# Decode attention on one core: keys transposed in place four groups at a time, and one load of the last value tile split by partitions

## The chip, the core and the metric

The kernel runs on one core of a Trainium2 chip. A core has a matrix engine (TensorE, PE in the profile, its weight loads PEld), a vector engine (VectorE, DVE), a scalar engine (ScalarE, ACT), GpSimd (POOL), and a queue engine (SyncE, SP) that here only issues transfers. Sixteen DMA engines move data between HBM and the on-chip memory SBUF, which has 128 partitions. The metric is the time of one execution in microseconds, taken as the median of several runs.

## The reference

One query token attends to 65,536 keys. There are 32 query heads and 8 key/value heads, so that four query heads share one key/value head; a head has 128 numbers, and everything is bf16.

```python
B, Hq, Hkv, Sq, Sk, D = 1, 32, 8, 1, 65536, 128
scores = jnp.einsum("bhqd,bhkd->bhqk", q, k) * D ** -0.5
p = softmax(scores, axis=-1)
out = jnp.einsum("bhqk,bhkd->bhqd", p, v)
```

Keys and values are 134 MB each. Each is read once, and there is little arithmetic for a byte.

## The kernel before

The outer loop runs over the key/value heads g. The 65,536 rows of a head are laid out so that partition p holds rows 512p to 512p+511. They come in four tiles (s = 0 to 3) of 128 rows for each partition, 4 MB a tile. A tile is one transfer: `k_load` (L118) and `v_load` (L196) each issue it from the SP queue. All tiles, of keys and of values, share one pool of four buffers (`iopool`), so a tile's load waits until the work on the tile four places earlier has let go of its buffer.

`k_step` (L124) computes the scores of one key tile. The 128 rows of a partition are seen as 16 chunks c of 8 groups w; the group w takes every eighth row. VectorE transposes blocks of 32 by 32 four-byte words, two groups in an instruction, out of the key tile `kn` into a tile `T` from a pool of three (L133 to L138). Four matmuls for each group (L144) read `T`; the 32 matmuls of a tile add up in one PSUM bank `sc`, which ScalarE copies out (L151). Since only the transposes read `kn`, the key buffer comes free when the last of the four transposes of a tile is done.

`softmax` (L153) follows the fourth key tile of a head: VectorE takes a maximum, TensorE and VectorE spread it, and ScalarE computes the exponentials. `transpose_weights` (L187) turns them on VectorE. The values of head g-1 are multiplied by them while the keys of head g come in: `v_stream` (L206) has 32 matmuls for a value tile, behind the 32 matmuls of the key tile in TensorE's queue. So the loads alternate between keys and values, except for four key tiles at the beginning and four value tiles at the end.

The last value tile is loaded in six pieces, of 64, 32, 16, 8, 4 and 4 rows for each partition, so that `finish_last` (L262) can work on a piece while the next one lands. After the last piece come a few small matmuls, one VectorE operation, and the store of 4 partitions, issued from ScalarE's queue (L250). There are two earlier stores of that kind, of 4 and of 3 rows for each of 4 partitions, and four loads of the queries of 32 partitions each (L70), on that queue too.

Buffers are given out, waits are put in and the order on each engine is chosen by a planner ahead of the run. It makes an instruction wait for an earlier one when their accesses to a tile conflict. Transfers count their completion on a rotation of semaphores.

Of the kernel before, what the change touches and what calls it, by code (L numbers as in the profile page):

```python
# [14 lines left out]
NW = 16  # L15
# [5 lines left out]
def kernel(  # L21
# [17 lines left out]
    nc = tc.nc  # L39
    P = nc.NUM_PARTITIONS  # L40
    B, Hq, Sq, D = q.shape
# [10 lines left out]
    fp32 = mybir.dt.float32  # L52
    bf16 = mybir.dt.bfloat16

    const = ctx.enter_context(tc.tile_pool(name="const", bufs=1))
    iopool = ctx.enter_context(tc.tile_pool(name="iopool", bufs=4))
    tpool = ctx.enter_context(tc.tile_pool(name="tpool", bufs=3))
    spool = ctx.enter_context(tc.tile_pool(name="spool", bufs=2))
    epool = ctx.enter_context(tc.tile_pool(name="epool", bufs=2))
    opool = ctx.enter_context(tc.tile_pool(name="opool", bufs=2))  # L60
# [14 lines left out]
    for x in range(2):  # L75
# [8 lines left out]
        out=sel[:, :], in_=ident[:, :].rearrange("p (x h) -> p h x", h=HPG), axis=AX.X, op=ALU.max  # L84
# [3 lines left out]
        out=blk[:, :], in_=ident[:, :].rearrange("p (j w h) -> p w j h", w=W, h=HPG), axis=AX.XY, op=ALU.max  # L88
# [35 lines left out]
    def k_step(g, s, kn):  # L124
        if s == 0:
            S_tiles[g] = spool.tile([P, KT, 4 * P], fp32, name="S_g")
        wq = Wq[g % 2]
        kv = kn[:, :, :].rearrange("p (c w) d -> p w c d", w=W)
        sc = psc.tile([P, 4 * P], fp32, name="sc")
        for w in range(W):  # L130
            if s == 0 and w == W // 2 and g > 0:
                transpose_weights(g - 1)
            if w % 2 == 0:  # L133
                T = tpool.tile([P, 2, NW, D], bf16, name="T")
                nc.vector.transpose(  # L135
                    out=T[:, :, :, :].bitcast(fp32),
                    in_=kv[:, w:w + 2].bitcast(fp32),
                )  # L138
            Tv = T[:, w % 2].rearrange("p n (b i r) -> p n b i r", b=2, r=2)
            for b in range(2):  # L140
                for r in range(2):
                    bp = 2 * b + r
                    at = bp * WX + 28 - 4 * w
                    nc.tensor.matmul(  # L144
                        out=sc[:, :],
                        lhsT=wq[:, at:at + P],
                        rhs=Tv[:, :, b, :, r],
                        start=(w == 0 and bp == 0),
                        stop=(w == W - 1 and bp == 3),
                    )  # L150
        nc.scalar.copy(out=S_tiles[g][:, s, :], in_=sc[:, :])  # L151
# [35 lines left out]
    def transpose_weights(g):  # L187

        ET = epool.tile([P, KT, NW, 32], bf16, name="ET")
        nc.vector.transpose(  # L190
            out=ET[:, :, :, :].rearrange("p s c x -> p (s c x)"),
            in_=E_tiles[g][:, :, :].rearrange("p s x -> p (s x)"),
        )
        ET_tiles[g] = ET

    def v_load(g, s, pieces=(NT,)):  # L196
        vb = iopool.tile([P, NT, D], bf16, name="vb", tag="io", align_bytes=2048)
        src = v[0, g].rearrange("(p n) d -> p n d", p=P)
        x = 0
        for step in pieces:  # L200
            n0 = s * NT + x
            nc.sync.dma_start(out=vb[:, x:x + step, :], in_=src[:, n0:n0 + step, :])  # L202
            x += step
        return vb

# [94 lines left out]
    for g in range(Hkv + 1):  # L300
        if 0 < g < Hkv:
            queries(g)
        for s in range(KT):
            if g < Hkv:
                k_step(g, s, k_load(g, s))
            elif s == 0:
                transpose_weights(g - 1)
            if g > 0:
                last = s == KT - 1
                if g == Hkv and last:  # L310
                    finish_last(g - 1, s, v_load(g - 1, s, pieces=(64, 32, 16, 8, 4, 4)))
                else:
                    v_stream(g - 1, s, v_load(g - 1, s), NT, last)
                    if last:
                        pick(g - 1)
                    if last and g % 4 == 0:
                        finish(g - 4, 4)
                    if last and g == Hkv - 1:
                        finish(g - g % 4, g % 4)
        if g < Hkv:  # L320
            softmax(g)
# [30 lines left out]
```

## Time and profile before

| | us |
|---|---|
| median of 3 runs | 631.95 (631.68 to 632.71) |
| profiled execution, its own time | 632.0 |
| profiled execution, span from first to last instruction | 630.1 |
| DMA, mean rate over the span | 427 GB/s |
| TensorE busy, share of the span | 58% |
| VectorE busy, share of the span | 54% |
| mean granted TensorE clock | 0.783 |

The span leaves out 1.9 us of the execution's own time. In the rows of instruction groups, a line names the source line, the engine, the operation, what it writes and reads, and the shape with the number of instructions; behind the bar stand busy time, the mean of one in nanoseconds, and the idle time ahead of them with what ended it. In the rows of stretches, the columns are the stretch and its length, busy time of five engines, the granted clock, the share of the DMA engines' time, and the rate.

### The profile page before, as it was taken

What the parts mean: (1) busy time and instruction counts of PE and PEld (TensorE: products, weight loads), DVE (VectorE), ACT (ScalarE), POOL (GpSimd) and SP (SyncE); (2) the same over time, 40 slices, a digit from 0 to 9 for tenths busy, and PEclk for the clock granted to TensorE, in tenths of its full rate; (3) what the DMA queues carried; (4) which work ended last, traced back from release to release, by engine and by line L of the source; (5) the groups of instructions that cost most, each with busy time, mean ns of one, the idle gap of its engine ahead of it and who ended that gap; (6) DMA issues with size and microseconds to landing.
All of it is one profiled execution on the core that took longest, in us unless ns stands there. A gap on an engine that the chain in (4) does not pass through costs nothing.

```text
span 630.1 us, 4872 instructions
## 1 busy us (share of the span) xinstructions
PE 363.2 (58%) x2134; PEld 141.8 (23%) x2134; DVE 340.0 (54%) x200; ACT 36.8 (6%) x49; POOL 6.4 (1%) x37
## 2 busy tenths in 40 slices
PE   0686836745457464575645856457665466644645
PEld 0232312212122221222211222112221122211212
DVE  0998834784337753377543675336754366553511
ACT  0000100010000100001000010001000010000100
POOL 0000000000000000000000000000000000000000
PEclk9998888767787677876778867788677787767866
DMA  8999999999999999999999999999999999999996
GB/s 368 433 434 431 433 432 431 432 433 433 434 433 432 435 433 434 433 432 433 434 435 435 432 427 432 437 432 433 433 432 433 434 433 433 432 433 434 431 425 263
DMA packets 10192, 268.78 MB, mean 427 GB/s; under 512 B 1340, under 2 KB 1596, under 8 KB 1852
## 3 DMA queue, kind: packets, MB, share of 16 engines
q1 hardware_dynamic: 9936, 268.44, 98.9%
q8 instruction: 16, 0.26, 0.1%
q10 hardware_dynamic: 236, 0.04, 0.0%
q14 instruction: 4, 0.03, 0.0%
HBM read 268.47 MB, written 0.01 MB: 426 GB/s over the span
## 4 chain that ended last, share of the span: by engine, by line
DMA 73%; DVE 11%; issue 10%; PE 4%; ACTq 0%; DVEq 0%; SPq 0%
DMA kn<-in_k_dram 66%; DVE T L135 11%; DMA vb<-in_v_dram 5%; PE sc L144 4%; DMA qn<-in_q_dram 2%; PE psum_o L213 0%; ACTq L70 0%; DVEq L135 0%; PE psum_f L280 0%; PE psum_oT L290 0%; SPq L202 0%; DVE wq L109 0%; PE psum_f L287 0%; PE psum_f L296 0%; DVE sel L83 0%
## 5 line engine op out<-in xcount | busy, mean ns | idle before, releaser
L144 PE MATMUL sc<-T,wq 128*128 128x512 bf16 x1024 | 288.1, 445 | 220.3 <-DVE T L135 220.3
L135 DVE STREAM_TRANSPOSE T<-kn 128x2048 f32<-128x2048 f32 x128 | 284.2, 2277 | 198.2 <-DMA kn<-in_k_dram 198.2
L144 PEld LDWEIGHTS <-wq 128*128 128x128 bf16 x1024 | 109.4, 109 | 394.9 <-issue 159.6
L213 PE MATMUL psum_o<-vb,ET 128*32 128x512 bf16 x1008 | 64.8, 402 | 12.3 <-DMA vb<-in_v_dram 10.1
L151 ACT COPY S_g<-sc 128x512 f32<-128x512 f32 x32 | 18.8, 587 | 511.0 <-PE sc L144 511.0
L213 PEld LDWEIGHTS <-ET 128*32 128x32 bf16 x1008 | 25.5, 100 | 49.2 <-issue 28.2
L156 DVE TENSOR_REDUCE mx<-S_g 128x1 f32<-128x2048 f32 x8 | 18.3, 2286 | 26.7 <-ACT S_g L151 26.7
L190 DVE STREAM_TRANSPOSE ET<-E_g 128x2048 bf16<-128x2048 bf16 x8 | 18.5, 2311 | 16.3 <-ACT E_g L177 16.3
L177 ACT ACTIVATE E_g<-S_g,nmb 128x2048 bf16<-128x2048 f32 x8 | 16.0, 2001 | 47.5 <-DVE nmb L174 40.4
L224 DVE TENSOR_TENSOR o_m<-psum_o,mask 128x512 f32<-128x512 f32 x8 | 5.5, 681 | 21.5 <-PE psum_o L213 21.5
L109 POOL COPY wq<-qx 32x16 bf16<-32x16 bf16 x28 | 5.3, 190 | 427.2 <-PE sc L144 410.2
L160 PE MATMUL psum_t<-ident,mx 128*1 128x128 f32 x8 | 2.2, 270 | 11.2 <-DVE mx L156 11.2
L100 DVE STREAM_TRANSPOSE qx<-qn 128x64 f32<-128x64 f32 x1 | 0.2, 245 | 15.2 <-DMA qn<-in_q_dram 15.2
L172 PE MATMUL psum_b<-one,mrow 1*128 1x1 f32 x16 | 3.6, 290 | 8.3 <-DVE mrow L166 8.3
L230 DVE TENSOR_REDUCE o_all<-o_m 128x128 f32<-128x512 f32 x8 | 8.0, 1000 | 0.0
L172 PEld LDWEIGHTS psum_b<-one,mrow 1*128 1x128 f32 x16 | 3.0, 235 | 12.1 <-issue 11.3
L237 PE MATMUL psum_l<-lsum_all,sel 128*4 128x4 f32 (+2 forms) x6 | 0.6, 166 | 7.7 <-ACT E_g L177 7.7
L257 PE MATMUL psum_f<-o_all,sel 128*4 128x512 f32 (+1 forms) x4 | 2.4, 705 | 2.9 <-DVE o_all L230 2.9
L160 PEld LDWEIGHTS psum_t<-ident,mx 128*1 128x1 f32 x8 | 0.6, 79 | 15.1 <-DVE mx L156 11.6
L244 DVE TENSOR_TENSOR o_out<-psum_f,rl 4x512 bf16<-4x512 f32 (+2 forms) x3 | 1.5, 501 | 3.6 <-PE psum_f L257 2.4
L290 PE MATMUL psum_oT<-ET,vb 128*128 128x4 bf16 x56 | 2.0, 167 | 1.6 <-DMA vb<-in_v_dram 1.6
L174 DVE COPY nmb<-psum_b 128x1 f32<-128x1 f32 x8 | 1.2, 152 | 3.0 <-PE psum_b L172 3.0
(28 smaller groups left out, 16.0 us busy)
## 6 DMA issues: line engine op xcount, KB each, us to landing
kn<-in_k_dram SPq DMA_DIRECT2D x32, 4096.0 KB, 29.6
vb<-in_v_dram SPq DMA_DIRECT2D x31, 4096.0 KB, 34.5
vb<-in_v_dram SPq DMA_DIRECT2D x1, 2048.0 KB, 29.5
vb<-in_v_dram SPq DMA_DIRECT2D x1, 1024.0 KB, 31.5
vb<-in_v_dram SPq DMA_DIRECT2D x1, 512.0 KB, 32.3
vb<-in_v_dram SPq DMA_DIRECT2D x1, 256.0 KB, 32.4
vb<-in_v_dram SPq DMA_DIRECT2D x2, 128.0 KB
qn<-in_q_dram ACTq DMA_DIRECT2D x4, 8.0 KB, 10.3
```

Source lines behind the costliest of these rows:

```text
L109: eng.tensor_copy(out=wv[qd, :, :, 32 * a + 28:32 * a + 28 + HPG], in_=qv[qd, :, :, g * HPG:(g + 1) * HPG],)
L135: nc.vector.transpose(out=T[:, :, :, :].bitcast(fp32), in_=kv[:, w:w + 2].bitcast(fp32),)
L144: nc.tensor.matmul(out=sc[:, :], lhsT=wq[:, at:at + P], rhs=Tv[:, :, b, :, r], start=(w == 0 and bp == 0), stop=(w == W - 1 and bp == 3),)
L151: nc.scalar.copy(out=S_tiles[g][:, s, :], in_=sc[:, :])
L156: nc.vector.tensor_reduce(out=mx[:, :], in_=S_g[:, :, :].rearrange("p n c -> p (n c)"), axis=AX.X, op=ALU.max)
L160: nc.tensor.transpose(out=psum_t[:, :], in_=mx[:, :], identity=ident[:, :])
L172: nc.tensor.matmul(out=psum_b[:, :], lhsT=mrow[:, :], rhs=one[:, :], start=True, stop=True)
L177: nc.scalar.activation(out=E_g[:, :, :].rearrange("p s x -> p (s x)"), in_=S_g[:, :, :].rearrange("p s x -> p (s x)"), func=ACT.Exp, bias= ...
L190: nc.vector.transpose(out=ET[:, :, :, :].rearrange("p s c x -> p (s c x)"), in_=E_tiles[g][:, :, :].rearrange("p s x -> p (s x)"),)
L213: nc.tensor.matmul(out=o_tiles[g][32 * j:32 * j + 32, :, :], lhsT=ET_tiles[g][:, s, c, :], rhs=vb[:, c * W + 4 * x:c * W + 4 * x + 4, :], ...
L224: nc.vector.tensor_tensor(out=o_m[:, :, :], in0=o_tiles[g][:, :, :], in1=mask[:, :].unsqueeze(2).broadcast_to([P, 4, D]), op=ALU.mult,)
L230: nc.vector.tensor_reduce(out=o_all[:, g, :], in_=o_m[:, :, :].rearrange("p x d -> p d x"), axis=AX.X, op=ALU.add)
```

## The change

The pool of `T` tiles goes. VectorE transposes four groups of a key tile in one instruction and writes them where it read them; the matmuls read the key tile itself. In the last value tile, the piece of 32 rows is loaded by five transfers in place of one: partitions 0 to 111, and then 112 to 115, 116 to 119, 120 to 123 and 124 to 127. No other transfer has 32 rows.

```diff
-    tpool = ctx.enter_context(tc.tile_pool(name="tpool", bufs=3))
...
         for w in range(W):
             if s == 0 and w == W // 2 and g > 0:
                 transpose_weights(g - 1)
-            if w % 2 == 0:
-                T = tpool.tile([P, 2, NW, D], bf16, name="T")
-                nc.vector.transpose(
-                    out=T[:, :, :, :].bitcast(fp32),
-                    in_=kv[:, w:w + 2].bitcast(fp32),
-                )
-            Tv = T[:, w % 2].rearrange("p n (b i r) -> p n b i r", b=2, r=2)
+            if w % 4 == 0:
+                groups = kv[:, w:w + 4].bitcast(fp32)
+                nc.vector.transpose(out=groups, in_=groups)
+            Tv = kv[:, w].rearrange("p n (b i r) -> p n b i r", b=2, r=2)
...
         for step in pieces:
             n0 = s * NT + x
-            nc.sync.dma_start(out=vb[:, x:x + step, :], in_=src[:, n0:n0 + step, :])
+
+            p0 = 0
+            for p1 in (112, 116, 120, 124, P) if step == 32 else (P,):
+                nc.sync.dma_start(out=vb[p0:p1, x:x + step, :], in_=src[p0:p1, n0:n0 + step, :])
+                p0 = p1
             x += step
```

## The prediction

> **What bounds the kernel now.** I read the rows of slices first, then the waits of the SP queue, then the groups, then the last microseconds.
>
> ```profile
> DMA  8999999999999999999999999999999999999996
> GB/s 368 433 434 431 433 432 431 432 433 433 434 433 432 435 433 434 433 432 433 434 435 435 432 427 432 437 432 433 433 432 433 434 433 433 432 433 434 431 425 263
> ```
>
> The DMA engines are busy in every slice, at 433 GB/s from the second on. 268.4 MB at 433 GB/s is 620 us of the 630.1 us span. Around it lie the first 1.7 us and the work after the last piece. So time is lost only by a hole in this stream, or at its end.
>
> ```profile
> L144 PE MATMUL sc<-T,wq 128*128 128x512 bf16 x1024 | 288.1, 445 | 220.3 <-DVE T L135 220.3
> L135 DVE STREAM_TRANSPOSE T<-kn 128x2048 f32<-128x2048 f32 x128 | 284.2, 2277 | 198.2 <-DMA kn<-in_k_dram 198.2
> ...
> kn<-in_k_dram SPq DMA_DIRECT2D x32, 4096.0 KB, 29.6
> vb<-in_v_dram SPq DMA_DIRECT2D x31, 4096.0 KB, 34.5
> ```
>
> VectorE idles 198.2 us for keys, so it isn't the bound. A 4 MB tile takes 9.7 us at 433 GB/s, yet a key load lands 29.6 us after its issue: two more tiles stand ahead of it in the queue. That is the cover for the first edit.
>
> ```profile
> 621.00:622.00 1.00, 0.94 (x16) 0.35 (x15) 0.00 (x0) 0.00 (x0) 0.00 (x0) 1.00 0.97 400
> 622.00:623.00 1.00, 0.10 (x4) 0.00 (x0) 0.81 (x2) 0.00 (x0) 0.00 (x0) 0.90 0.91 360
> 623.00:624.00 1.00, 0.51 (x19) 0.51 (x20) 0.90 (x1) 0.00 (x0) 0.00 (x0) 0.50 0.62 250
> 624.00:625.00 1.00, 0.79 (x29) 0.71 (x27) 0.00 (x0) 0.00 (x0) 0.00 (x0) 0.50 0.54 205
> 625.00:626.00 1.00, 1.00 (x22) 0.56 (x18) 0.00 (x0) 0.00 (x0) 0.00 (x0) 0.50 0.30 105
> ```
>
> The DMA share falls to a half before it falls to nothing: the engines don't end together. By the packets, seven end between 622.8 and 623.2 us, one at 624.6 and eight near 625.6. The second edit works on this.
>
> ```profile
> 592.38 32.29 DMA vb<-in_v_dram
> 624.67 0.05 issue
> 624.72 0.58 PE psum_oT L290 x16
> 625.30 0.52 PE psum_f L287 x2
> 625.82 0.30 PE psum_oT L290 x8
> 626.12 0.52 PE psum_f L280 x4
> ```
>
> In the chain that ended last, the piece of 16 rows lands at 624.7 us; from there TensorE's work follows without a gap. What delays that landing delays the end by as much.
>
> **Edit 1, transposes in place.** 128 instructions of 2.28 us go and 64 of twice the size come. Back to back the old ones stand 2.2 us apart (four in 8.89 us), so a new one takes about 4.4 us, from at least 2.3 us (no more than an old one) to 4.6 us (two old ones). VectorE's load of 284 us stays or falls a little: worth nothing, as its idle time is 198 us.
>
> What moves is when a key buffer comes free: no longer after the last transpose, but after the last matmul. At 188.8 us the four transposes take 8.9 us and the buffer is free at 197.7 us. After the change, 4.4 us + 4.4 us + 16 matmuls of 0.30 us (32 took 9.55 us) make 13.6 us: free at 202.4 us, 4.7 us later. Behind this load on SP stands the value load, whose buffer TensorE frees 1.9 us later. The next two loads give cover: a key load must reach the queue before the three tiles landing after its predecessor in the buffer are through, some 28 us after that one landed, and 14 us are used. Where a head begins, the weights' transpose (2.3 us) and the wait for exponentials add about 5 us, leaving 9 us. Tightest is the start: VectorE works through four key tiles until 53.5 us; then comes the first softmax. Two transposes and the maximum, each waited for, put the fifth tile's last matmul near 73.4 us instead of the release at 67.7 us. The load into its buffer must be moving at 80 us, when the three tiles behind the fifth are in; with 1.0 us from issue to moving 5.7 us are left. Cost: nothing. If that cover went, each microsecond beyond it would be a microsecond of DMA.
>
> The matmuls now read rows 2 KB apart instead of 256 bytes. No row shows this; bounded by equal speed and by the 631 ns that a value matmul takes at the half clock instead of 445 ns, a tile's 32 need 9.6 to 13.6 us, with 1.9 us of value matmuls still under the 19.4 us of two loads. I take equal speed, since the transposes already read this pitch at the rate of the packed ones. Cost: nothing either way.
>
> **Edit 2, five transfers for one.** SP issues four more, 0.43 us each, 1.7 us, about 20 us ahead of need. Completions go round eight semaphores, and a transfer waits for the one eight places before it:
>
> ```profile
> SPq L202 <- DMA out_dram<-o_out: 7.1, 1, 7.1
> SPq L202 <- DMA vb<-in_v_dram: 3.8, 2, 3.5
> ```
>
> With ten transfers for the last tile the ninth waits for the 64-row piece (621.1 us) and the tenth for the 112-partition transfer. A wake takes 0.4 us and an issue reaches the engines 1.0 us later, while a late engine has 2.2 us of 16, 8 and 4 rows left: 0.8 us of cover, cost nothing; without it, the shortfall.
>
> Engines: in the before, 236 packets stand on ScalarE's queue.
>
> ```profile
> q10 hardware_dynamic: 236, 0.04, 0.0%
> ```
>
> The query loads have 128 rows and the stores 16 + 12 + 4; 236 - 160 leaves 76 completions, which is 4 loads by 16 and 3 stores by 4. So a transfer of 4 partitions runs on four engines. Three of those are among the early seven and one is the engine that ends at 624.6 us (by the packets of the store at 600 us). At 433/16 = 27.1 GB/s for an engine, 8 KB take 0.31 us. The twelve others lose one packet in eight: -0.3 us. The four get 11 packets for 8: +0.9 us, so the one in between ends at 625.5 us. Best case: end 0.1 to 0.3 us earlier.
>
> That holds if the parts keep the full rate of every engine; no row has a transfer of 112 partitions or a large one of 4. The other end: the four small transfers, 128 KB, go at the rate of a single engine, 4.8 us, in place of 1.2 us: +3.6 us on top. The one in between, 1.0 us ahead, then ends 3.5 us late; the early three, 2.5 to 2.8 us ahead, 1.7 to 2 us late. If moreover the 112 partitions went at 205 GB/s, the rate with half the engines at work, their 0.92 MB would take 4.5 us for 2.1 us: +2.4 us, 5.9 us in all. Between -0.3 and +5.9 us I take +3.0 us, nearer the engine's rate than the full one: the only 4-partition transfers in the trace already leave twelve engines out. Sum: 632.0 + 0 + 3.0 = 635.0 us for the profiled execution, which stands at the median (631.95).
>
> [...]
>
> **The rivals.** *The tail stays as it is* (0.30): every engine keeps 27.1 GB/s whatever partitions it writes. For it: all engines run alike in 63 tiles. [...] Time 631.8 us. It decides as long as the small transfers lose less than 1.4 us on the engine in between, which ends at 625.5 us: beyond that the end is more than 1.3 us late.
>
> *The second transposes wait for the first 16 matmuls* (0.07), if the planner takes the interleaved groups for one region. The place is the second transpose of each key tile; a tile then takes 4.4 + 4.9 + 4.4 + 4.9 = 18.6 us on VectorE and TensorE in turn, decisive from 19.4 us on. At a head's start 4.6 us of maximum and weights come on top. 18.3 + 4 x 16.4 (full clock) + 28 x 18.6 + 7 x 4.6 + 25 us for the last values = 662 us.
>
> *Faster* (0.03): the engines even out. The mean of their ends is 624.3 us: at most 1.3 us, 630.7 us.
>
> **How the numbers follow.** Likeliest, with 0.60, is the split that costs: 635.0 us, own range 633.3 to 638. A change under 0.2% (1.3 us) can't be told from none here. Same 0.30, slower 0.60 + 0.07, faster 0.03. The range 631.5 to 638.2 leaves out the waiting transposes, the gain and the worst end.
>
> **What would show it.** The transpose row at 64 of about 4.4 us; key loads landing about 25 us after issue; DMA slices at 433 GB/s until 615 us; then a tail in which the DMA share sinks for longer and the 16-row piece lands near 628 us. I am wrong if slices before 600 us dip, if the transposes wait for matmuls, or if the tail ends at 625.5 us.

## The result, and the profile after

The changed kernel takes 636.86 us, the median of six runs, against 632.13 us for the kernel before. Five of the six lie between 635.97 and 637.12 us; the sixth, a disturbed one of 711.25 us, is not counted in the ratio, which is 1.0072 with a 95% interval of 1.0061 to 1.0084. The profiled execution took 636.67 us, its span is 634.9 us. So 4.7 us were lost, where 3.0 us had been forecast.

Over most of the span nothing changed. The slices of the changed kernel:

```profile
DMA  9999999999999999999999999999999999999996
GB/s 370 440 442 428 436 428 429 428 429 428 429 429 429 448 441 429 429 428 429 428 431 433 440 440 433 431 428 429 429 430 436 433 442 435 431 429 428 432 415 147
```

The rate stays near 433 GB/s up to slice 38 and there is no hole; only the last two slices are poorer, 415 and 147 instead of 425 and 263 GB/s. The groups and the landing of the key loads show that the first edit did what it says:

```profile
L140 PE MATMUL sc<-kn,wq 128*128 128x512 bf16 x1024 | 286.4, 445 | 224.0 <-DVE kn L134 222.8
L134 DVE STREAM_TRANSPOSE kn<-kn 128x4096 f32<-128x4096 f32 x64 | 280.2, 4418 | 189.9 <-DMA kn<-in_k_dram 189.9
...
kn<-in_k_dram SPq DMA_DIRECT2D x32, 4096.0 KB, 24.0
```

64 transposes take 4.42 us each, 280 us together for 284 us before. A matmul takes 445 ns as before. The key loads land 24.0 us after issue instead of 29.6 us: they are issued later, and the queue ahead of them is still longer than one tile.

The loss lies in the last 18 us. Stretches of the kernel before (first fence) and of the changed one (second); the last two columns are the share of the DMA engines' time and the rate:

```profile
616.00:618.00 2.00, 1.80 (x20) 0.82 (x23) 0.00 (x0) 0.00 (x0) 0.00 (x0) 0.50 0.91 389
618.00:620.00 2.00, 1.66 (x20) 0.56 (x13) 0.00 (x0) 0.00 (x0) 0.00 (x0) 0.66 1.12 477
620.00:622.00 2.00, 0.94 (x16) 0.35 (x15) 0.00 (x0) 0.00 (x0) 0.00 (x0) 1.00 0.88 362
```

```profile
616.00:618.00 2.00, 1.50 (x16) 0.69 (x19) 0.00 (x0) 0.00 (x0) 0.00 (x0) 0.50 0.97 414
618.00:620.00 2.00, 2.00 (x20) 0.70 (x13) 0.00 (x0) 0.00 (x0) 0.00 (x0) 0.50 1.08 266
620.00:622.00 2.00, 0.10 (x4) 0.00 (x0) 0.00 (x0) 0.00 (x0) 0.00 (x0) 0.78 1.21 219
622.00:624.00 2.00, 0.00 (x0) 0.00 (x0) 0.00 (x0) 0.00 (x0) 0.00 (x0) 1.00 0.75 168
624.00:626.00 2.00, 1.47 (x16) 0.49 (x15) 0.00 (x0) 0.00 (x0) 0.00 (x0) 0.57 0.99 188
626.00:628.00 2.00, 0.43 (x4) 0.00 (x0) 1.49 (x2) 0.00 (x0) 0.00 (x0) 0.50 0.81 198
```

From 618 us on, the engines are busy and move half as much. Packet by packet the same is seen: in the kernel before, every packet of 8 KB near the end takes 309 ns; in the changed one they take 0.31 to 1.09 us, mostly near 0.6 us. The 64-row piece, a transfer that was not changed, has 128 packets of 16 KB; 35 of them rise in the same microseconds from 611 ns to between 0.80 and 1.77 us.

TensorE, in order of time, first before and then after:

```profile
621.06 1.05 PE L213 MATMUL psum_o<-vb,ET 128*32 128x512 bf16 x16 [1.40 <-DMA vb<-in_v_dram]
623.49 1.01 PE L290 MATMUL psum_oT<-ET,vb 128*128 128x4 bf16 x32 [1.39 <-DMA vb<-in_v_dram]
624.72 0.58 PE L290 MATMUL psum_oT<-ET,vb 128*128 128x4 bf16 x16 [0.21 <-DMA vb<-in_v_dram]
```

```profile
624.53 1.90 PE L213 MATMUL psum_o<-vb,ET 128*32 128x512 bf16 x16 [4.43 <-DMA vb<-in_v_dram]
628.96 1.42 PE L290 MATMUL psum_oT<-ET,vb 128*128 128x4 bf16 x48 [2.53 <-DMA vb<-in_v_dram]
```

The 64-row piece is there 3.5 us later, the 32-row piece 5.5 us later. The last packet of the 16-row piece ends at 629.2 us, while the matmuls of the 32 rows run, so the 48 matmuls of both go without a gap. From there the work is the same as before.

### The profile page after: what moved, and what is told of

Read it like the earlier page. It is cut to its first block, busy times and chain, and to the rows that moved or that the text cites. A ratio compares the mean times of both kernels' runs of the same rounds, so it can differ in the third digit from the quotient of the medians.

```text
span 634.9 us, 4750 instructions
## 1 busy us (share of the span) xinstructions
PE 361.7 (57%) x2134; PEld 141.8 (22%) x2134; DVE 336.3 (53%) x136; ACT 36.8 (6%) x49; POOL 6.4 (1%) x37
## 3 DMA queue, kind: packets, MB, share of 16 engines
q1 hardware_dynamic: 9952, 268.44, 99.0%
## 4 chain that ended last, share of the span: by engine, by line
DMA 63%; PE 22%; DVE 14%; issue 0%; ACTq 0%; DVEq 0%; SPq 0%
DMA kn<-in_k_dram 55%; PE sc L140 21%; DVE kn L134 14%; DMA vb<-in_v_dram 5%; DMA qn<-in_q_dram 2%; PE psum_o L213 0%; PE psum_oT L290 0%; ACTq L69 0%; PE psum_f L280 0%; DVE wq L108 0%; PE psum_f L287 0%; PE psum_f L296 0%; DVE sel L82 0%; DVEq L134 0%; SPq L201 0%
## 5 line engine op out<-in xcount | busy, mean ns | idle before, releaser
L140 PE MATMUL sc<-kn,wq 128*128 128x512 bf16 x1024 | 286.4, 445 | 224.0 <-DVE kn L134 222.8
L134 DVE STREAM_TRANSPOSE kn<-kn 128x4096 f32<-128x4096 f32 x64 | 280.2, 4418 | 189.9 <-DMA kn<-in_k_dram 189.9
L213 PEld LDWEIGHTS <-ET 128*32 128x32 bf16 x1008 | 25.3, 100 | 53.3 <-issue 29.6
```

The lines of the kernel that those rows point to most:

```text
L134: nc.vector.transpose(out=groups, in_=groups)
L140: nc.tensor.matmul(out=sc[:, :], lhsT=wq[:, at:at + P], rhs=Tv[:, :, b, :, r], start=(w == 0 and bp == 0), stop=(w == W - 1 and bp == 3),)
L213: nc.tensor.matmul(out=o_tiles[g][32 * j:32 * j + 32, :, :], lhsT=ET_tiles[g][:, s, c, :], rhs=vb[:, c * W + 4 * x:c * W + 4 * x + 4, :], ...
```

## The experiments

Three accounts were to be told apart. By the first, the split is the whole cost, since the parts of a split transfer hinder each other where they are written into SBUF; that is a supposition, as the trace shows no packet's partition. By the second, the cost is one of counts: more transfers, and later ones that wait for the completion of earlier ones. By the third, the transposes in place carry a part of it, since they hold the key buffers longer. All kernels were compared with the kernel before on the same chip.

**Each edit alone.** The first kernel has the transposes in place and the one transfer of before; the second has separate `T` tiles and the split.

```diff
 e1_inplace, against the changed kernel
-            p0 = 0
-            for p1 in (112, 116, 120, 124, P) if step == 32 else (P,):
-                nc.sync.dma_start(out=vb[p0:p1, x:x + step, :], in_=src[p0:p1, n0:n0 + step, :])
-                p0 = p1
+            nc.sync.dma_start(out=vb[:, x:x + step, :], in_=src[:, n0:n0 + step, :])
```

> The transposes in place alone; the 32-row piece is one transfer of 128 partitions again. My theory (the split is the whole cost): the time of the kernel before within 0.2%, 631.5 to 633.0 us, with the DMA rate in the last microseconds as before (324 to 477 GB/s between 616 and 622 us). Rival (a part of the loss comes from the buffers held longer, which may make loads late): 633.5 us or more, with slices under 430 GB/s well before the tail.

> The split of the 32-row piece alone; the transposes write into separate tiles as before. My theory: the whole loss, 636 to 637.5 us, with packets of 8 KB near 0.6 us instead of 0.31 us and a tail at about 200 to 270 GB/s between 618 and 628 us although the engines are busy. Rival (in-place transposes carry part of it): below 635.5 us.

The first took 631.79 us, 0.9999 of the kernel before (0.9990 to 1.0008). The second took 636.68 us, 1.0075 (1.0063 to 1.0088). The third account falls, and the first edit is worth nothing measurable in either direction. The tail of the second kernel has the half rate with busy engines again:

```profile
618.00:620.00 2.00, 1.73 (x19) 0.50 (x9) 0.00 (x0) 0.00 (x0) 0.00 (x0) 0.54 1.04 246
620.00:622.00 2.00, 0.00 (x0) 0.00 (x0) 0.00 (x0) 0.00 (x0) 0.00 (x0) 1.00 1.11 186
622.00:624.00 2.00, 0.00 (x0) 0.00 (x0) 0.00 (x0) 0.00 (x0) 0.00 (x0) 0.81 0.87 184
```

**The same count, split by rows.** Five transfers of the same sizes, but of all 128 partitions each:

```diff
-            p0 = 0
-            for p1 in (112, 116, 120, 124, P) if step == 32 else (P,):
-                nc.sync.dma_start(out=vb[p0:p1, x:x + step, :], in_=src[p0:p1, n0:n0 + step, :])
-                p0 = p1
-            x += step
+            for r in (28, 1, 1, 1, 1) if step == 32 else (step,):
+                nc.sync.dma_start(out=vb[:, x:x + r, :], in_=src[:, n0:n0 + r, :])
+                x += r
+                n0 += r
```

> The changed kernel, but the 32-row piece is split by rows: five transfers of 28, 1, 1, 1 and 1 rows, each of all 128 partitions. [...] If partitions that two engines write at once are the cause: 632 to 633 us, the tail at full rate. If the number of transfers or the waits of the later ones are the cause: 636 us or more.

632.00 us, 1.0004 (0.9994 to 1.0014). The tail is at the full rate:

```profile
618.00:620.00 2.00, 1.56 (x16) 0.50 (x9) 0.00 (x0) 0.00 (x0) 0.00 (x0) 0.66 0.99 410
620.00:622.00 2.00, 1.05 (x16) 0.36 (x15) 0.05 (x1) 0.00 (x0) 0.00 (x0) 1.00 1.01 396
```

The second account falls: five transfers in place of one, and the waits that come with them, cost nothing here.

**Which of the five.** Two kernels change the four small transfers. One gives each of them every fourth partition in place of four neighbours; one makes a single transfer of them.

```diff
 e4_stride
...
+                nc.sync.dma_start(out=vb[0:112, x:x + step, :], in_=src[0:112, n0:n0 + step, :])
+                for j in range(4):
+                    nc.sync.dma_start(out=vb[112 + j:P:4, x:x + step, :], in_=src[112 + j:P:4, n0:n0 + step, :])
...
 e5_112_16
-            for p1 in (112, 116, 120, 124, P) if step == 32 else (P,):
+            for p1 in (112, P) if step == 32 else (P,):
```

> The changed kernel, but the four small transfers take every fourth partition: 112, 116, 120, 124, then 113, 117, 121, 125, and so on. [...] If the four small transfers' shared group of partitions is the larger part of the loss: 633 to 634.5 us. If the transfer of 112 partitions is: 635.5 to 637 us, nearly as the change. If partitions don't matter: 636.9 us, as the change.

> The changed kernel with one transfer of 16 partitions (112 to 127) in place of four of 4. [...] If uneven bytes among the engines were the cost: 632 us.

636.71 us, 1.0078 (1.0062 to 1.0093), and 637.23 us, 1.0079 (1.0064 to 1.0094). Neither is better than the change. So it is not the larger part of the loss that the partitions of a small transfer are neighbours, nor that the small transfers are four; but both kernels still load the last 16 partitions apart from the others, so they alone do not clear the small transfers. What both also have in common with the change is the transfer of 112 partitions.

**The parts by themselves.** In the next three the 32-row piece is unsplit, and work is added behind it: loads into a tile that nothing reads.

```diff
...
+            nc.sync.dma_start(out=vb[:, x:x + step, :], in_=src[:, n0:n0 + step, :])
+            if step == 32:
+                more = const.tile([P, 32, D], bf16, name="more")
 e8_more128
+                nc.sync.dma_start(out=more[:, 0:28, :], in_=src[:, n0:n0 + 28, :])
 e7_more112
+                nc.sync.dma_start(out=more[0:112, :, :], in_=src[0:112, n0:n0 + step, :])
 e6_more4
+                for p0 in (112, 116, 120, 124):
+                    nc.sync.dma_start(out=more[p0:p0 + 4, :, :], in_=src[p0:p0 + 4, n0:n0 + step, :])
```

> Transposes in place, the 32-row piece unsplit, and behind it one more transfer, of 28 rows in all 128 partitions (0.92 MB) into a tile that nothing reads: work is added, the output is untouched. It is the control of the next run. At 433 GB/s the addition is 2.1 us: 633.9 us.

> The same, but the added transfer has 32 rows in partitions 0 to 111: the same 0.92 MB. If its engines write into each other's groups of partitions and lose rate for it: 636 to 639 us, with packets near 0.6 us. If only the bytes count: 633.9 us, as the control.

> The same with four added transfers of 4 partitions (112 to 127, 32 rows, 0.13 MB) in place of the 112. If the four small transfers are no large part of the loss, as the run with every fourth partition says: 632 to 633.3 us. If each of them goes at the rate of one engine: 634 us or more.

The control adds 2.3 us (634.29 us; 1.0032, 1.0019 to 1.0044), about what its bytes need (0.92 MB at 433 GB/s: 2.1 us). The same bytes in 112 partitions add 6.3 us (638.33 us; 1.0098, 1.0083 to 1.0113). The difference, 4.0 us, is the price of the form at this place. The four small ones add 1.15 us (633.14 us; 1.0019, 1.0010 to 1.0028) for a seventh as many bytes, which need 0.3 us at 433 GB/s. In the same two stretches, the control and then the 112 partitions:

```profile
622.00:624.00 2.00, 0.61 (x19) 0.32 (x12) 1.62 (x2) 0.00 (x0) 0.00 (x0) 0.85 0.99 413
624.00:626.00 2.00, 0.70 (x27) 0.61 (x24) 0.10 (x1) 0.00 (x0) 0.00 (x0) 0.50 0.85 337
```

```profile
622.00:624.00 2.00, 0.14 (x4) 0.00 (x0) 1.71 (x2) 0.00 (x0) 0.00 (x0) 0.81 0.98 184
624.00:626.00 2.00, 0.00 (x0) 0.00 (x0) 0.00 (x0) 0.00 (x0) 0.00 (x0) 0.50 1.02 236
```

**The cause by itself.** So far HBM could still be the place, as another form reads HBM in another order. Three kernels add a load of the same 96 rows of the same 16 value partitions, and only the 16 partitions written differ.

```diff
...
+            nc.sync.dma_start(out=vb[:, x:x + step, :], in_=src[:, n0:n0 + step, :])
+            if step == 32:
+                more = const.tile([P, 96, D], bf16, name="more")
 e10_own
+                nc.sync.dma_start(out=more[32:96:4, :, :], in_=src[0:16, 0:96, :])
 e11_pairs
+                nc.sync.dma_start(out=more[0:64:4, :, :], in_=src[0:16, 0:96, :])
 e12_fours
+                nc.sync.dma_start(out=more[0:16, :, :], in_=src[0:16, 0:96, :])
```

> Transposes in place, the 32-row piece unsplit, and behind it one more transfer, of 96 rows of 16 value partitions (0.39 MB) into a tile that nothing reads; the output is untouched. The rows read in HBM are the same in this run and the next two; only the 16 partitions written differ. Here they are 32, 36, 40, up to 92. [...] If any transfer of 16 partitions is slow: 635 us or more.

> [...] If HBM or the count of partitions set the rate, the same time as the two others.

> [...] If HBM or the count of partitions set the rate, the same time as the two others.

| partitions written | time, us | ratio | added, us | mean of a 24 KB packet, ns |
|---|---|---|---|---|
| 32, 36, ... 92 | 632.61 | 1.0008 (0.9998 to 1.0017) | 0.5 | 912 |
| 0, 4, ... 60 | 634.39 | 1.0033 (1.0019 to 1.0047) | 2.3 | 1343 |
| 0 to 15 | 636.50 | 1.0068 (1.0053 to 1.0083) | 4.4 | 2086 |

The added time is that over the kernel before, 632.07 us on that chip. The time goes with the partitions written, as the first account supposes, and not with their count, which is 16 in all three. 912 ns for 24,576 bytes is 27 GB/s, a sixteenth of the 433 GB/s of the stream. The packets of the others are 1.5 and 2.3 times as long in the mean. They don't start together: with partitions 0 to 15, eight of the sixteen packets start by 621.0 us and the other eight not before 624.3 us. The rows read in HBM were the same and the time differed, so for these transfers the place is the write into SBUF. The stretch from 622 to 624 us, first with partitions 32 to 92, then with 0 to 15:

```profile
622.00:624.00 2.00, 1.44 (x33) 0.68 (x26) 1.15 (x2) 0.00 (x0) 0.00 (x0) 0.50 0.90 357
```

```profile
622.00:624.00 2.00, 1.05 (x16) 0.36 (x15) 0.69 (x1) 0.00 (x0) 0.00 (x0) 1.00 0.86 245
```

**In mid-stream.** Is it a matter of the tail, with its small pieces? One kernel splits four whole value tiles, of heads 2 to 5.

```diff
 e9_mid, against the changed kernel
+            parts = {(2, 1): (112, 116, 120, 124, P), (3, 1): (64, P), (4, 1): (112, P), (5, 1): (120, P)}.get((g, s), (P,))
             p0 = 0
-            for p1 in (112, 116, 120, 124, P) if step == 32 else (P,):
+            for p1 in parts:
                 nc.sync.dma_start(out=vb[p0:p1, x:x + step, :], in_=src[p0:p1, n0:n0 + step, :])
                 p0 = p1
```

> Transposes in place, the last tile unsplit; four value tiles in mid-stream, each 4 MB, are split by partitions: 112 and four times 4 (head 2), 64 and 64 (head 3), 112 and 16 (head 4), 120 and 8 (head 5). If colliding engines halve the rate, each of the four shows a dip to about 220 GB/s with the engines busy, and each costs 5 to 12 us that nothing hides: 655 to 680 us. If the loss belongs to the tail alone (small pieces, engines ending apart), the slices stay at 430 GB/s and the time at 632 to 634 us.

721.13 us in its one run: the direction was right, the size was missed. By the count of packets that had ended, against the kernel with the transposes in place alone, the stream fell back by 16.0 us at the tile of 112 and four times 4, by 23.4 us at 64 and 64, 19.8 us at 112 and 16, and 20.6 us at 120 and 8; some 9 us more fell later, and their cause was not looked for. A tile needs 9.7 us, so half the rate for one tile would cost 9.7 us more. Before, within and after the split into 64 and 64:

```profile
300.00:310.00 10.00, 3.77 (x43) 1.61 (x41) 5.47 (x7) 2.68 (x3) 0.76 (x4) 0.84 0.99 429
320.00:330.00 10.00, 6.90 (x54) 2.71 (x52) 0.00 (x0) 0.59 (x1) 0.00 (x0) 0.98 0.95 141
330.00:340.00 10.00, 0.00 (x0) 0.10 (x1) 2.33 (x1) 0.00 (x0) 0.00 (x0) 0.53 0.98 205
340.00:350.00 10.00, 7.83 (x24) 2.93 (x24) 6.44 (x2) 0.00 (x0) 0.00 (x0) 0.61 1.08 190
360.00:370.00 10.00, 2.97 (x28) 1.00 (x21) 1.17 (x1) 0.00 (x0) 0.00 (x0) 0.50 1.03 442
```

The engines are busy throughout, and for 30 us they move less than half. The loss is not bound to the tail. It is also larger than half the rate for one tile would make it, and no run shows why. At 120 and 8, by the count of packets, the engines also have unequal shares: SP's queue has 9,991 packets against 9,936, 55 more, of which the other three tiles make 48 if each of their splits adds sixteen; that leaves 23 completions for the two parts in place of 32.

## Why the prediction was right, and where it was not

**Edit 1, cost nothing.** Right, in each step that the trace shows. The transposes take 4.42 us (4.4 us was taken), the matmuls that now read rows 2 KB apart take 445 ns as before, and the key loads land 24.0 us after issue, which leaves more than a tile ahead of them. The kernel with this edit alone shows 0.9999. The tightest place was safer than reckoned: the fifth tile's buffer was free at 68.4 us and not at 73.4 us.

**The waits on eight semaphores, cost nothing.** Right. The last two pieces were issued at 624.5 us and 628.7 us, each on the landing of the transfer eight places earlier:

```profile
SPq L201 <- DMA vb<-in_v_dram: 24.3, 5, 9.5
SPq L201 <- DMA out_dram<-o_out: 7.8, 1, 7.8
```

TensorE did not wait for them after 628.96 us, and the split by rows, which has the same waits, took the time of the kernel before.

**Engines of a 4-partition transfer.** The count of completions gave four engines. The changed kernel bears it out: SP's queue has 9,952 packets against 9,936 before, 16 more, which is four completions for each of the four small transfers if the 112 partitions have sixteen, like the piece before. That the same four engines serve all four small transfers, and so have three packets more than before, was an estimate; no run shows it. A transfer of 16 partitions is not held to four engines: that into partitions 32 to 92, 0.39 MB, added 0.5 us, where four engines at 27.1 GB/s would need 3.6 us. The kernel with a single transfer of 16 in place of the four is no faster than the change (637.23 us), so the few engines of the small transfers are not what the change costs.

**The sum of the split, +3.0 us between -0.3 and +5.9.** The side was right and so was the reason, that parts of a split transfer don't keep the full rate; the size was low, 4.8 us by the split alone (636.68 over 631.88 us). The step that failed is the share of the two terms. I charged the four small transfers with up to 3.6 us and made the 112 partitions an afterthought of up to 2.4 us. It is the other way round: 4.0 us for the form of the 112 partitions, and 1.15 us for four small transfers added by themselves, 0.3 us of them for their bytes. That a small transfer goes at the rate of a single engine, from which the 3.6 us came, was an estimate that no run shows. That 635.0 us still came within 2 us of the result is in part luck: a price too high for the small transfers made up for part of one too low for the 112 partitions. The bound for the 112 had only their own bytes at 205 GB/s. It left out the transfer ahead: 35 of the 128 packets of the unchanged 64-row piece took 0.80 to 1.77 us in place of 611 ns, and that piece alone came 3.5 us late. The gain of 0.3 us on twelve engines never appeared.

**What would show it.** The slices to 615 us and the landing of the keys came as said. The 16-row piece was expected near 628 us; it was the 32-row piece that landed then (628.7 us) and held both. That the DMA share would sink for longer was wrong: from 618 to 628 us it stayed between 0.75 and 1.21, and the rate sank. Busy engines had been read as working engines.

**The rivals.** That the tail would stay was refuted by the split alone; that the second transposes would wait for matmuls, by the edit alone; a gain did not come.

What stays open is how 112 partitions are dealt to sixteen engines, since a packet's partition is not in the trace. So that the 112 partitions lose their rate in the same way as the 16 is inferred; what is shown is that their form costs 4.0 us over the same bytes in 128 partitions.

## What to carry to other kernels

In a stream bound by DMA, split a transfer by rows and leave it all 128 partitions: five such transfers in place of one cost nothing here (632.00 us against 631.88 us), while splits by partitions cost 4.8 us for a piece of 1 MB in the tail and 16 to 23 us for one tile of 4 MB. Look at the rate beside the engines' busy share: busy engines need not be working engines (a share of 1.21 at 219 GB/s between 620 and 622 us). One transfer of 16 partitions in place of four of 4 did not help here (637.23 us). That a buffer comes free later cost nothing here, since the queue still held more than one load, which the time from issue to landing shows (24.0 us against 9.7 us for a load).

## What the runs showed of the hardware that was not expected

A transfer of 16 partitions can have packets at the rate that an engine has in the stream (24 KB in 912 ns, 27 GB/s): 0.39 MB into partitions 32 to 92 by fours cost 0.5 us, the same bytes into 0 to 15 cost 4.4 us. Between these runs the choice of partitions, not their number, set the price.

A split reaches beyond its own transfer. The unchanged 64-row piece ahead of it landed 3.5 us later, and in mid-stream a tile that needs 9.7 us held the stream up by as much as 23.4 us.
